# Attention tokens staged in natural order, one transfer per head, with the last 64 tokens of all heads in one transfer

## The chip, the core and the metric

The kernel runs on one core of a Trainium2 chip. The core has a matrix engine (PE, with its weight loads shown apart as PEld), a vector engine (DVE), a scalar engine for activations (ACT), a general engine (POOL), a sync engine that issues transfers (SP), and 16 DMA engines that every queue shares. Each engine works through its own instructions in the order in which they were written, and waits on semaphores of the others. The metric is the device time of one execution in microseconds.

## The reference

Two stages follow each other. Forgetting attention for 8 batches of 8 heads, 576 tokens and head size 64:

```
scores = (q @ k.T) / sqrt(64)
cum    = cumsum(log(clip(f, 1e-4, 1)))           # per head, over tokens
scores = where(causal, scores + cum[i] - cum[j], -1e9)
attn   = softmax(scores);  a = attn @ v
```

The heads are then put side by side (4608 tokens of 512), and go through a normalised gated feed-forward without biases:

```
xn  = x / sqrt(mean(x*x) + 1e-6) * rms_g
out = (silu(xn @ w_gate) * (xn @ w_val)) @ w_out       # 512 -> 1536 -> 512
```

All inputs and the output are float32.

## The kernel before

A batch is worked in four pairs of heads. Its 576 tokens are cut into five blocks, four of 128 and one of 64. For a pair, q and k of the first 512 tokens lie in `q32` and `k32` as [128, 2 heads, 4, 64], loaded so that partition p holds the four neighbouring tokens 4p to 4p+3, which is one run of 1 KB in memory for each head. The last 64 tokens of q and k lie in `r32` (q on partitions 0 to 63, k on 64 to 127), v in `v32` in natural order, partition p holding tokens p, 128+p and so on, in runs of 256 B. There are four sets of these tiles (NST = 4), so that a pair is loaded one batch ahead.

`cast` (L166) turns q, the rest and k into bfloat16 (`qkb`), on DVE in the first batch and on POOL in the others, and then issues the loads of the pair four further on. `scale_v` (L176) multiplies v with the decay factor of each key on POOL into `Vs`, and issues v's loads of the pair four further on. `transposes` (L187) turns the nine blocks of a pair with PE into one PSUM tile `tr`, in two parts, five blocks with the rest and then four of k; the tile exists once (`ps_tr` has one buffer), so the next transposes of any kind wait until DVE has copied it. That copy is L199: since block e holds every fourth token, it writes the 512 columns in the order (m e) while it reads them as (e m), with a stride of four in its destination. L202 copies the rest plainly, and two POOL copies (L204) build a block-diagonal matrix `QB` from it.

`scores` then multiplies q and k (L211), ACT exponentiates (L247), POOL masks (L215), and `values` multiplies with `Vs` (L273); DVE divides by the row sums (L276, L277) into `x`. The tile `po`, which holds these results and the scores of the last block (L225), also exists once. `squares` on ACT (L287), `root` on POOL (L293, L295), `normed` on DVE (L304) and `transpose_x` (L310 on PE, L317 on DVE, through the same `tr` tile) prepare the feed-forward. That is `gate` (L383, L386, L387), `value` (L393, L395) and `project` (L404, L410, store at L412), in groups of 512 tokens.

What sets the order is the function `order`: it issues the first batch alone, and after it a fixed list of the attention work of batch b+1 is dealt out among the feed-forward work of batch b, by counting. No engine reorders it. The decay factors come first: `decay_sums` (L144) clips f on DVE, takes the logarithm on ACT, scans on DVE and exponentiates on ACT; `decay_columns` (L153) transposes the result on PE, and DVE copies it to `decT`, which `scale_v` needs.

Transfers are issued on three queues. SP issues f, q and k, the later v and all stores of the output; ACT issues v of the first three pairs ahead of its first activation; POOL issues the weights, with a cast to bfloat16 on the way.

## Time and profile before

| | us |
|---|---|
| median of 2 runs | 504.88 |
| the runs | 502.15, 507.6 |
| the profiled execution | 507.5 |
| its span, from first to last instruction | 505.8 |

Its span by stage, from the busy time in windows:

| stage (us from the start) | PE busy | DVE busy | POOL busy | granted PE clock | DMA share |
|---|---|---|---|---|---|
| 0 to 12.6, first loads and decay | 0.00 | 4.09 | 0.73 | 1.00 | 0.83 |
| 12.6 to 57, batch 0 alone (two windows) | 23.98 | 26.27 | 25.07 | 1.00 | 0.79, 0.81 |
| 57 to 131, batch 0's feed-forward with batch 1 (two windows) | 59.78 | 47.01 | 36.19 | 1.00, 0.90 | 0.70, 0.57 |
| 185 to 239, a batch in mid-kernel | 46.54 | 34.92 | 21.84 | 0.94 | 0.31 |
| 294 to 346, another | 44.25 | 35.29 | 21.84 | 1.00 | 0.32 |
| 431 to 460, feed-forward alone | 28.95 | 17.54 | 0.00 | 1.00 | 0.10 |

Rows of the profile read thus. A group of instructions has its line, engine, operation, tiles (out<-in), shape and count, then busy time in all and the mean of one in ns, then the idle time of that engine just ahead of it and who ended it. In the chain of waits each line is a start, a duration and what ran; the chain is followed back from the last instruction to whatever released each step. A timeline row has start, duration, engine, line and operation, and in brackets the idle time before it with its releaser. Busy PE time is modelled, since matmuls are pipelined; a PE that idles is shown by its brackets.

### The profile page before, as it was taken

How to read it: one execution, taken by the hardware profiler on the slowest of the kernel's cores; microseconds unless marked ns; L12 is line 12 of the kernel's file. 1: busy time of each engine (PE TensorE's matmuls, PEld its weight loads, DVE VectorE, ACT ScalarE, POOL GpSimd, SP SyncE). 2: the span in 40 equal slices, each digit the busy share in tenths (PEclk: the TensorE clock that was granted, in tenths of full speed). 3: DMA queues.
4: the chain of work that ended last, by engine and by line, in shares of the span. 5: the costliest groups of instructions: out<-in, count | busy, mean ns of one | idle time of the engine just before them, and what ended most of it. 6: DMA issues, size and time to landing. Idle time of an engine off the chain costs nothing.

```text
span 505.8 us, 8861 instructions
## 1 busy us (share of the span) xinstructions
PE 414.6 (82%) x3317; PEld 205.5 (41%) x3317; DVE 312.7 (62%) x576; ACT 215.6 (43%) x354; POOL 175.7 (35%) x377
## 2 busy tenths in 40 slices
PE   0564677796989789879987898969897899999997
PEld 0343334343444344434443444434443444444443
DVE  3863487745686557773787368655866567374570
ACT  1443144562446235533546154634472454232331
POOL 0562636744344316351645034442544111000000
PEclk9999999997999799989999799999998999999999
DMA  8797839643052314331232305231000100201102
GB/s 214 197 204 125 163 91 189 164 116 113 25 138 72 92 62 128 86 93 56 80 112 60 103 25 139 71 113 43 2 0 23 64 1 0 85 0 38 46 2 83
DMA packets 75595, 43.20 MB, mean 85 GB/s; under 512 B 49888, under 2 KB 70880, under 8 KB 75552
## 3 DMA queue, kind: packets, MB, share of 16 engines
q1 hardware_dynamic: 67216, 37.03, 26.5%
q0 software_dynamic: 4736, 4.72, 6.0%
q10 hardware_dynamic: 3600, 0.89, 0.8%
q8 instruction: 26, 0.43, 0.3%
q14 instruction: 17, 0.14, 0.1%
HBM read 37.90 MB, written 9.44 MB: 94 GB/s over the span
## 4 chain that ended last, share of the span: by engine, by line
PE 56%; DVE 21%; ACT 10%; issue 6%; POOL 3%; DMA 2%; SPq 1%; POOLq 0%; ACTq 0%; DVEq 0%
PE bg L404 17%; PE bg L383 14%; PE bg L393 12%; DVE QK L199 5%; ACT junk L287 5%; PE po L273 5%; DVE th L387 4%; PE bg L211 4%; DVE xn L304 3%; ACT th L386 3%; DVE x L277 3%; DVE hT L395 3%; PE tr L310 3%; PE tr L194 1%; ACT PT L247 1%
## 5 line engine op out<-in xcount | busy, mean ns | idle before, releaser
L247 ACT ACTIVATE PT<-bg 128x1024 bf16<-128x1024 f32 x96 | 98.0, 1022 | 53.1 <-PE bg L211 52.9
L387 DVE SCALAR_TENSOR_TENSOR th<-th,bg 128x512 f32<-128x512 f32 x108 | 73.8, 683 | 63.9 <-ACT th L386 63.4
L393 PE MATMUL bg<-xT,wv 128*128 128x512 bf16 x432 | 113.0, 385 | 0.0
L404 PE MATMUL bg<-wo,hT 128*128 128x512 bf16 x432 | 111.6, 406 | 1.7 <-DVE hT L395 1.1
L383 PE MATMUL bg<-xT,wg 128*128 128x512 bf16 x432 | 112.8, 384 | 0.0
L386 ACT ACTIVATE th<-bg 128x512 f32<-128x512 f32 x108 | 64.4, 597 | 113.0 <-PE bg L383 113.0
L199 DVE COPY QK<-tr 128x512 bf16<-128x512 bf16 x64 | 83.0, 1297 | 11.3 <-PE tr L197 10.1
L395 DVE SCALAR_TENSOR_TENSOR hT<-th,bg 128x512 bf16<-128x512 f32 x108 | 74.4, 689 | 16.6 <-PE bg L393 9.0
L215 POOL TENSOR_SCALAR_AFFINE_SELECT PT<-PT 128x256 bf16<-128x256 bf16 (+1 forms) x96 | 46.6, 486 | 81.3 <-ACT PT L247 80.4
L404 PEld LDWEIGHTS <-hT 128*128 128x128 bf16 x432 | 41.7, 103 | 53.3 <-issue 11.8
L317 DVE TENSOR_SCALAR xT<-tr,rg 128x512 bf16<-128x512 bf16 (+7 forms) x64 | 20.6, 364 | 61.0 <-PE tr L310 61.0
L393 PEld LDWEIGHTS <-wv 128*128 128x128 bf16 x432 | 38.4, 99 | 43.7 <-issue 7.1
L194 PE MATMUL tr<-ident,qkb 128*128 128x128 bf16 x256 | 26.7, 231 | 35.7 <-DVE qkb L170 13.6
L383 PEld LDWEIGHTS <-wg 128*128 128x128 bf16 x432 | 37.9, 99 | 37.3 <-issue 1.7
L410 ACT COPY ores<-bg 128x512 f32<-128x512 f32 x36 | 21.1, 586 | 61.5 <-PE bg L404 61.5
L273 PEld LDWEIGHTS <-PT 128*128 128x128 bf16 x896 | 38.6, 104 | 19.3 <-POOL PT L215 5.2
L211 PE MATMUL bg<-QK 64*128 64x64 bf16 (+3 forms) x576 | 40.7, 251 | 0.0
L310 PE MATMUL tr<-ident,xn 128*128 128x128 bf16 x160 | 17.3, 243 | 28.0 <-DVE QK L199 19.5
L194 PEld LDWEIGHTS <-qkb 128*128 128x128 bf16 x256 | 18.7, 102 | 49.1 <-issue 21.8
L277 DVE TENSOR_TENSOR x<-po,rden 128x320 f32<-128x320 f32 x64 | 31.5, 492 | 2.2
L211 PEld LDWEIGHTS <-QK 64*128 64x128 bf16 x576 | 17.0, 98 | 28.6 <-issue 24.7
L310 PEld LDWEIGHTS <-xn 128*128 128x128 bf16 x160 | 12.8, 107 | 36.4 <-issue 21.7
(106 smaller groups left out, 323.4 us busy)
## 6 DMA issues: line engine op xcount, KB each, us to landing
out_dram<-ores SPq DMA_DIRECT2D x36, 256.0 KB, 2.0
q_0_103<-in_q_dram SPq DMA_DIRECT2D x8, 256.0 KB, 2.7
k_0_107<-in_k_dram SPq DMA_DIRECT2D x8, 256.0 KB, 3.2
q_1_104<-in_q_dram SPq DMA_DIRECT2D x8, 256.0 KB, 3.2
k_1_108<-in_k_dram SPq DMA_DIRECT2D x8, 256.0 KB, 3.3
q_2_105<-in_q_dram SPq DMA_DIRECT2D x8, 256.0 KB, 2.9
k_2_109<-in_k_dram SPq DMA_DIRECT2D x8, 256.0 KB, 3.4
q_3_106<-in_q_dram SPq DMA_DIRECT2D x8, 256.0 KB, 2.8
```

What stands on the lines that cost most here:

```text
L194: nc.tensor.transpose(tp[:, e * 128:(e + 1) * 128], src[:, 5 * part + e, :, :].rearrange("p h d -> p (h d)"), ident)
L199: nc.vector.tensor_copy(t[:, c:c + 512].rearrange("k (m e) -> k e m", e=4), tp[:, 0:512].rearrange("k (e m) -> k e m", e=4))
L211: nc.tensor.matmul(sc[:, par, c:c + n], lhsT=QK[b, p][rows, KEYS[kj]:KEYS[kj] + 128], rhs=QK[b, p][rows, q0:q0 + n], start=True, stop=True)
L247: nc.scalar.activation(t, sc, ACT.Exp, scale=scale)
L273: nc.tensor.matmul(po[:, qi, :], lhsT=weights_of(b, h, qi, kj), rhs=Vs[b % 2][:, kj, h, :], start=(kj == 0), stop=(kj == qi))
L277: nc.vector.tensor_tensor(xs[b][:, :, h * D:(h + 1) * D], po[:, :, 0:D], bcast(r[:, :], D), ALU.mult)
L383: nc.tensor.matmul(pg, lhsT=wg[:, dc, fc * 128:(fc + 1) * 128], rhs=xTs[g][:, dc, :], start=(dc == 0), stop=(dc == NDC - 1))
L386: readers[g, fc] = (nc.scalar.activation(t, pg, ACT.Tanh, scale=0.5), nc.vector.scalar_tensor_tensor(t, in0=t, scalar=1.0, in1=pg, op0=ALU ...
L387: nc.vector.scalar_tensor_tensor(t, in0=t, scalar=1.0, in1=pg, op0=ALU.add, op1=ALU.mult))
L393: beside(nc.tensor.matmul(pv, lhsT=wv[:, dc, fc * 128:(fc + 1) * 128], rhs=xTs[g][:, dc, :], start=(dc == 0), stop=(dc == NDC - 1)), reade ...
L395: nc.vector.scalar_tensor_tensor(hT, in0=ths.pop((g, fc)), scalar=0.5, in1=pv, op0=ALU.mult, op1=ALU.mult)
L404: beside(nc.tensor.matmul(po, lhsT=hTs[g, fc][:, j * 128:(j + 1) * 128], rhs=wo[:, fc, :], start=(fc == 0), stop=(fc == NFC - 1)), readers ...
```

## The change

Four things change together. q and k are loaded like v, in natural order: partition p holds tokens p, 128+p, 256+p and 384+p, in runs of 256 B, with one transfer for each head where there was one for a pair. The last 64 tokens of all eight heads come in one transfer for each of q, k and v (`load_last`), into `r32` and `s32`, of which there are two sets, one per batch in turn. v of the first batch is issued by POOL's queue and no longer by ACT and SP. And all loads of a pair are issued together behind its `scale_v`. With the tokens in natural order, a part's transposed blocks are copied out of PSUM by one plain copy of 640 or 512 columns. `scale_v` has one product per pair, and one more per batch for the last tokens of all heads. In `order`, the first pair's cast goes ahead of the decay sums and the second pair's behind the first V scaling.

```diff
--- before.py
+++ after.py
@@ -75,35 +75,38 @@
 
     q32 = [consts.tile([128, 2, 4, D], F32, name=f"q32_{i}") for i in range(NST)]
     k32 = [consts.tile([128, 2, 4, D], F32, name=f"k32_{i}") for i in range(NST)]
-    r32 = [consts.tile([128, 2, D], F32, name=f"r32_{i}") for i in range(NST)]
-    v32 = [consts.tile([128, NB, 2, D], F32, name=f"v32_{i}") for i in range(NST)]
+    v32 = [consts.tile([128, 2, 4, D], F32, name=f"v32_{i}") for i in range(NST)]
+    r32 = [consts.tile([128, H, D], F32, name=f"r32_{i}") for i in range(2)]
+    s32 = [consts.tile([64, H, D], F32, name=f"s32_{i}") for i in range(2)]
     Vs = [consts.tile([128, NB, H, D + 1], BF16, name=f"Vs{i}") for i in range(2)]
     PT4 = [consts.tile([128, 2, 128], BF16, name=f"PT4_{i}") for i in range(3)]
 
     QB = [consts.tile([128, 128], BF16, name=f"QB_{i}") for i in range(3)]
 
-    def load_qk(n):
+    def load_pair(n, what="qkv"):
 
         b, h0, i = n // NP, 2 * (n % NP), n % NST
-        for src, dst, r in ((q, q32[i], 0), (k, k32[i], 64)):
-            nc.sync.dma_start(out=dst.rearrange("p h e d -> p h (e d)"),
-                              in_=src[b, h0:h0 + 2, 0:512, :].rearrange("h (p e) d -> p h (e d)", e=4))
-            nc.sync.dma_start(out=r32[i][r:r + 64, :, :],
-                              in_=src[b, h0:h0 + 2, 512:S, :].rearrange("h p d -> p h d"))
-
-    def load_v(n, eng=nc.sync):
-        b, h0, i = n // NP, 2 * (n % NP), n % NST
-        for h in range(2):
-            eng.dma_start(out=v32[i][:, 0:4, h, :],
-                          in_=v[b, h0 + h, 0:512, :].rearrange("(j p) d -> p j d", p=128))
-        eng.dma_start(out=v32[i][0:64, 4, :, :],
-                      in_=v[b, h0:h0 + 2, 512:S, :].rearrange("h p d -> p h d"))
+        for name, src, dst in (("q", q, q32[i]), ("k", k, k32[i]), ("v", v, v32[i])):
+            for h in range(2 * (name in what)):
+                eng = nc.gpsimd if name == "v" and b == 0 else nc.sync
+                eng.dma_start(out=dst[:, h, :, :], in_=src[b, h0 + h, 0:512, :].rearrange("(j p) d -> p j d", p=128))
+
+    def load_last(b, what="qkv"):
+        for name, src, dst in (("q", q, r32[b % 2][0:64, :, :]), ("k", k, r32[b % 2][64:128, :, :]), ("v", v, s32[b % 2])):
+            if name in what:
+                eng = nc.gpsimd if name == "v" and b == 0 else nc.sync
+                eng.dma_start(out=dst, in_=src[b, :, 512:S, :].rearrange("h p d -> p h d"))
 
     fr = consts.tile([BH, NB * 128], F32)
     nc.sync.dma_start(out=fr[:, 0:S], in_=f.rearrange("b h s -> (b h) s"))
-    for n in range(NP):
-        load_qk(n)
-        load_v(n, nc.scalar if n < 3 else nc.sync)
+    load_pair(0, "qk")
+    load_last(0, "qk")
+    load_pair(0, "v")
+    load_pair(1, "qk")
+    load_last(0, "v")
+    load_pair(1, "v")
+    load_pair(2)
+    load_pair(3)
     rg = consts.tile([128, NDC], F32)
     with nc.allow_non_contiguous_dma(reason="512 gains, once"):
         nc.sync.dma_start(out=rg, in_=moe_rms_g.rearrange("(c p) -> p c", p=128))
@@ -167,22 +170,24 @@
         i = (b * NP + p) % NST
         t = qkb[b, p] = qbp.tile([128, 9, 2, D], BF16, name="qkb")
         eng = nc.vector if b == 0 else nc.gpsimd
-        eng.tensor_copy(t[:, 0:4, :, :].rearrange("p e h d -> p h e d"), q32[i])
-        eng.tensor_copy(t[:, 4, :, :], r32[i])
-        eng.tensor_copy(t[:, 5:9, :, :].rearrange("p e h d -> p h e d"), k32[i])
-        if b * NP + p + NST < B * NP:
-            load_qk(b * NP + p + NST)
+        eng.tensor_copy(t[:, 0:4, :, :].rearrange("p j h d -> p h j d"), q32[i])
+        eng.tensor_copy(t[:, 4, :, :], r32[b % 2][:, 2 * p:2 * p + 2, :])
+        eng.tensor_copy(t[:, 5:9, :, :].rearrange("p j h d -> p h j d"), k32[i])
 
     def scale_v(b, p):
-        i, h0 = (b * NP + p) % NST, 2 * p
+        n, h0 = b * NP + p, 2 * p
         if b > 1 and p == 0:
             nc.gpsimd.tensor_copy(Vs[b % 2][:, :, :, D], decT[:, :, b * H:(b + 1) * H])
-        for rows, j0, j1 in ((128, 0, 4), (64, 4, 5)):
-            dj = decT[0:rows, j0:j1, b * H + h0:b * H + h0 + 2]
-            nc.gpsimd.tensor_tensor(Vs[b % 2][0:rows, j0:j1, h0:h0 + 2, 0:D],
-                                    v32[i][0:rows, j0:j1, :, :], bcast(dj, D), ALU.mult)
-        if b * NP + p + NST < B * NP:
-            load_v(b * NP + p + NST)
+        dj = decT[:, 0:4, b * H + h0:b * H + h0 + 2].rearrange("p j h -> p h j")
+        nc.gpsimd.tensor_tensor(Vs[b % 2][:, 0:4, h0:h0 + 2, 0:D].rearrange("p j h d -> p h j d"),
+                                v32[n % NST], bcast(dj, D), ALU.mult)
+        if p == 0:
+            nc.gpsimd.tensor_tensor(Vs[b % 2][0:64, 4, :, 0:D], s32[b % 2],
+                                    bcast(decT[0:64, 4, b * H:(b + 1) * H], D), ALU.mult)
+        if n + NST < B * NP:
+            load_pair(n + NST)
+        if p == 0 and b > 0 and b + 1 < B:
+            load_last(b + 1)
 
     def transposes(b, p, part):
 
@@ -190,16 +195,12 @@
             QK[b, p] = qkt.tile([128, 9 * 128], BF16, name="QK")
         t, src = QK[b, p], qkb[b, p]
         tp = ps_tr.tile([128, NB * 128], BF16, name="tr")
-        for e in range(4):
-            nc.tensor.transpose(tp[:, e * 128:(e + 1) * 128],
-                                src[:, 5 * part + e, :, :].rearrange("p h d -> p (h d)"), ident)
+        c0, c1 = ((0, 5), (5, 9))[part]
+        for c in range(c0, c1):
+            nc.tensor.transpose(tp[:, (c - c0) * 128:(c - c0 + 1) * 128],
+                                src[:, c, :, :].rearrange("p h d -> p (h d)"), ident)
+        nc.vector.tensor_copy(t[:, c0 * 128:c1 * 128], tp[:, 0:(c1 - c0) * 128])
         if part == 0:
-            nc.tensor.transpose(tp[:, 512:640], src[:, 4, :, :].rearrange("p h d -> p (h d)"), ident)
-        c = 640 * part
-        nc.vector.tensor_copy(t[:, c:c + 512].rearrange("k (m e) -> k e m", e=4),
-                              tp[:, 0:512].rearrange("k (e m) -> k e m", e=4))
-        if part == 0:
-            nc.vector.tensor_copy(t[:, 512:640], tp[:, 512:640])
             for r in (0, 64):
                 nc.gpsimd.tensor_copy(QB[(b * NP + p) % 3][r:r + 64, r:r + 64], t[r:r + 64, 512:576])
 
@@ -434,14 +435,15 @@
 
     def order():
 
+        cast(0, 0)
         decay_sums()
-        cast(0, 0)
         transposes(0, 0, 0)
         transposes(0, 0, 1)
-        cast(0, 1)
         decay_columns()
         scale_v(0, 0)
+        cast(0, 1)
         scale_v(0, 1)
+        load_last(1)
         for i, works in enumerate(attention(0)):
             run(works)
             if i in (11, 20):
```

How the instructions stand is shown with the names of the tiles: `tr` is the PSUM tile of transposes, `QK` its copy, `th` and `hT` belong to the feed-forward, `decT` holds the decay columns, numbers are those of tiles, and line numbers after the change are those of the changed file (L202 is there the copy from `tr`, L388 and L396 what were L387 and L395).

On DVE in mid-kernel, between two pairs' scores, before:

```order
L199 COPY QK<-tr 128x4x128
L202 COPY QK<-tr 128x128
L395 SCALAR_TENSOR_TENSOR hT<-th,bg 128x512
L387 SCALAR_TENSOR_TENSOR th<-th,bg 128x512
L199 COPY QK<-tr 128x4x128 x2
L202 COPY QK<-tr 128x128
L395 SCALAR_TENSOR_TENSOR hT<-th,bg 128x512
```

and after:

```order
L202 COPY QK<-tr 128x640
L396 SCALAR_TENSOR_TENSOR hT<-th,bg 128x512
L388 SCALAR_TENSOR_TENSOR th<-th,bg 128x512
L202 COPY QK<-tr 128x512
L202 COPY QK<-tr 128x640
L396 SCALAR_TENSOR_TENSOR hT<-th,bg 128x512
```

The places stay; the first part of a pair has one copy where it had two, and no copy reorders.

On DVE at the start, from the end of the decay sums to the decay columns, before:

```order
L150 TENSOR_SCALAR mid<-mid 64x1
L170 CAST qkb<-q_0_103 128x2x4x64
L171 CAST qkb<-r_0_111 128x128
L172 CAST qkb<-k_0_107 128x2x4x64
L199 COPY QK<-tr 128x4x128
L202 COPY QK<-tr 128x128
L199 COPY QK<-tr 128x4x128
L170 CAST qkb<-q_1_104 128x2x4x64
L171 CAST qkb<-r_1_112 128x128
L172 CAST qkb<-k_1_108 128x2x4x64
L158 COPY decT<-po 128x320
```

and after, from the last cast of the first pair to the first of the second:

```order
L175 CAST qkb<-k_0_107 128x2x4x64
L148 MEMSET fr 64x64
L149 TENSOR_SCALAR fr<-fr 64x576
L151 SCALAR_TENSOR_TENSOR cum<-one,fr 64x576
L152 TENSOR_TENSOR mid<-cum 64x1
L153 TENSOR_SCALAR mid<-mid 64x1
L202 COPY QK<-tr 128x640
L202 COPY QK<-tr 128x512
L161 COPY decT<-po 128x320
L163 CAST Vs_119<-decT 128x40
L163 CAST Vs_120<-decT 128x40
L173 CAST qkb<-q_1_104 128x2x4x64
```

The decay sums moved behind the first pair's cast, which waits for loads, and the decay columns ahead of the second pair's cast.

On POOL at the start, before:

```order
masks.py:199 AFFINE_SELECT ident_f<-ident_f 128x128
L204 COPY QB_124<-QK 64x64 x2
L182 TENSOR_TENSOR Vs_119<-v_0_115,decT 128x4x2x64
L182 TENSOR_TENSOR Vs_119<-v_0_115,decT 64x2x64
L182 TENSOR_TENSOR Vs_119<-v_1_116,decT 128x4x2x64
L182 TENSOR_TENSOR Vs_119<-v_1_116,decT 64x2x64
```

and after:

```order
L92 DMA v_0_111<-in_v_dram 128x4x64
masks.py:199 ISA
masks.py:199 AFFINE_SELECT ident_f<-ident_f 128x128
L92 DMA v_0_111<-in_v_dram 128x4x64
L98 DMA s_0_117<-in_v_dram 64x8x64
L92 DMA v_1_112<-in_v_dram 128x4x64 x2
L92 DMA v_2_113<-in_v_dram 128x4x64 x2
L92 DMA v_3_114<-in_v_dram 128x4x64 x2
L205 COPY QB_124<-QK 64x64 x2
L182 TENSOR_TENSOR Vs_119<-v_0_111,decT 128x2x4x64
L185 TENSOR_TENSOR Vs_119<-s_0_117,decT 64x8x64
L182 TENSOR_TENSOR Vs_119<-v_1_112,decT 128x2x4x64
```

Nine issues of v stand ahead of POOL's first copy, the first of them ahead of the identity that the transposes use.

## The prediction

> **What bounds the kernel now.** I read the page first, then the groups by line and shape, the busy time by stage, the chain of waits, and last the timeline of single engines around the gaps that the chain showed.
>
> ```profile
> span 505.8 us, 8861 instructions
> PE 414.6 (82%) x3317; PEld 205.5 (41%) x3317; DVE 312.7 (62%) x576; ACT 215.6 (43%) x354; POOL 175.7 (35%) x377
> PE 56%; DVE 21%; ACT 10%; issue 6%; POOL 3%; DMA 2%; SPq 1%; POOLq 0%; ACTq 0%; DVEq 0%
> L199 DVE COPY QK<-tr 128x512 bf16<-128x512 bf16 x64 | 83.0, 1297 | 11.3 <-PE tr L197 10.1
> ...
> 239.00:294.00 55.00, 47.53 (x399) 23.53 (x398) 35.87 (x68) 25.10 (x42) 21.84 (x47) 0.94 0.30 85
> ```
>
> PE is busiest, but only 56% of the chain is PE; 21% is DVE, at 62% busy. DVE isn't full: PE waits because DVE works its queue in order and something slow stands ahead of what PE needs. The costliest thing there for its size is L199, the eviction of the transposes that also reorders columns: 1.297 us for 512 columns. In the row of a batch in mid-kernel (columns: PE, PEld, DVE, ACT, POOL busy, clock, DMA share, GB/s) DMA engines are 0.30 busy.
>
> The chain of one such batch, thinned to its L199 pieces and to one mark per batch (start, us, what), then the first and last L199 pieces of the whole chain:
>
> ```profile
> 240.50 0.69 DVE th L387
> ...
> 295.15 0.69 DVE th L387
> 295.83 0.06 DVE QK L199
> 295.89 0.97 issue
> ...
> 311.92 1.21 DVE QK L199
> ...
> 318.44 0.06 DVE QK L199
> ...
> 326.67 1.30 DVE QK L199
> ...
> 332.43 1.21 DVE QK L199
> ...
> 347.36 0.69 DVE th L387
> ...
> 27.86 1.20 DVE QK L199
> ...
> 401.58 0.06 DVE QK L199
> ```
>
> Five L199 lie on the path in each batch. The "issue" of 0.97 behind 0.06 is the same instruction: the next one on DVE begins only when L199 makes room. A batch takes 347.36 - 295.15 = 52.2 us, the one before it 295.15 - 240.50 = 54.65.
>
> **The change part by part.**
>
> *The copy from PSUM.* Natural token order needs no reordering, so a pair has one plain copy of 128x640 and one of 128x512 in place of two L199 and one L202. No row shows these shapes as a copy; the nearest are:
>
> ```profile
> L202 DVE COPY QK<-tr 128x128 bf16<-128x128 bf16 x32 | 7.9, 247 | 0.0
> ...
> L317 DVE TENSOR_SCALAR xT<-tr,rg 128x512 bf16<-128x512 bf16 x8 | 3.8, 480 | 2.8 <-PE tr L310 2.8
> ...
> L317 DVE TENSOR_SCALAR xT<-tr,rg 128x64 bf16<-128x64 bf16 x8 | 2.0, 247 | 7.0 <-PE tr L310 7.0
> ```
>
> L317 reads the same kind of tile plainly: (480 - 247)/448 = 0.52 ns a column. From L202, 512 columns cost 247 + 384 x 0.52 = 447 ns and 640 cost 513. A pair falls from 2 x 1297 + 247 = 2841 to 960 ns; 32 pairs free 60 us of DVE. Bounds of the copy: 447 ns, and 1297 if the order of columns is not what makes it slow. I take 447, nearest in tile, type and engine.
>
> Only what lies on the path counts. I count 35 places on the chain: 2 up to 57 us, 7 from 57 to 131, 25 in the five batches to 400, one at 401.58. Each gives 1297 - 447 = 0.85 us (at 326.67 the L202 goes too, which pays for its longer copy): 35 x 0.85 = 29.75 us. Does the wait there shrink by as much? Three of the places end in these rows:
>
> ```profile
> 298.26 0.23 PE L225 MATMUL po<-QB_125,QK 128*128 128x128 bf16 x1 [0.93 <-DVE x L277]
> ...
> 313.17 0.38 PE L194 MATMUL tr<-ident,qkb 128*128 128x128 bf16 x4 [1.52 <-DVE QK L199]
> ...
> 333.68 0.44 PE L310 MATMUL tr<-ident,xn 128*128 128x128 bf16 x5 [3.14 <-DVE QK L199]
> ```
>
> PE idles 0.93, 1.52 and 3.14 us, each over 0.85, so PE's own work doesn't catch the gain. What is late next: at 298.26 PE itself, 0.08 us on; at 333.68 still DVE. I take all of it; half is the lower bound (a rival).
>
> *The clock behind the long gap.* Half the clock is granted after some gaps:
>
> ```profile
> 100.58 0.58 PE L194 MATMUL tr<-ident,qkb 128*128 128x128 bf16 x4 [2.38 <-DVE QK L199]
> ...
> 118.92 0.69 PE L310 MATMUL tr<-ident,xn 128*128 128x128 bf16 x5 [3.81 <-DVE QK L199]
> ...
> 100.50:103.50 3.00, 2.92 (x13) 1.17 (x13) 1.38 (x3) 1.02 (x1) 0.51 (x3) 0.50 0.59 146
> 278.70:284.70 6.00, 6.00 (x33) 3.12 (x33) 1.33 (x4) 0.28 (x1) 0.29 (x1) 0.52 0.38 102
> 333.70:339.00 5.30, 5.30 (x54) 3.01 (x54) 1.88 (x6) 1.89 (x3) 0.32 (x2) 1.00 0.45 128
> ```
>
> The windows give PE, PEld, DVE, ACT, POOL, clock, DMA share and GB/s. The gap before L310 comes six times, at 118.92 with 3.81 us and then with 3.14; behind it the clock falls to 0.5 in five (row at 278.70), not in one (333.70). An episode costs 54.65 - 52.2 = 2.45 us. A 2.38 us gap at 100.58 was followed by 0.50 too; the 1.52 us gap at 313.17 by none. After the change the gap of 3.14 becomes 3.14 - 0.85 = 2.29 (the earlier L199 at 326.67 moves both its ends). That is nearest to the 2.38 that did fall, so most episodes stay: I let one of five go, 2.45 us. The gap of 2.38 becomes 1.53, like the harmless 1.52; half of the 2.9 us at half clock, 1.4, is saved. Bounds: all five go, 12.25; or a sixth comes, -2.45. I take 2.45 + 1.4 = 3.85.
>
> *Loads.* q and k come as 256 B reads instead of 1 KB, four times as many; per pair seven issues become six, and three per batch carry the last tokens.
>
> ```profile
> q1 hardware_dynamic: 67216, 37.03, 26.5%
> q0 software_dynamic: 4736, 4.72, 6.0%
> q10 hardware_dynamic: 3600, 0.89, 0.8%
> ...
> wg<-in_moe_w_gate_dram POOLq DMA_DIRECT2D x3, 512.0 KB, 7.1
> ...
> fr<-in_f_dram SPq DMA_DIRECT2D x1, 144.0 KB, 3.5
> ...
> 3.00:6.00 3.00, 0.00 (x0) 0.00 (x0) 0.58 (x2) 0.00 (x0) 0.00 (x0) 1.00 0.98 245
> L127 POOL DMA_DIRECT2D wg<-in_moe_w_gate_dram x3 | 2.6, 868 | 0.0
> ```
>
> q10 carries almost only 256 B reads of v: 0.008 x 16 x 505.8/3600 = 18 ns each. q1's mean is 31.9 ns, q0's (casting) 102. The profile thus prices a read of 256 B at 18 to 31.9 ns. A batch has 8192 reads of q and k and 5632 others: 13824 x 18/16 = 15.6 us of all engines, 27.6 by q1's mean, under a period of 52.2 - 5 x 0.85 = 48 us. Each load is issued a whole batch ahead of its use, so I cost them at nothing; that cover is gone only when loads of a batch take longer than the batch. Their issue now stands behind the V scaling on POOL rather than the casts, some 1 to 2 us later: hidden too. On SP they and the stores of the output still share one queue, and 6.75 issues per pair are no more than 7.
>
> *POOL.*
>
> ```profile
> L182 POOL TENSOR_TENSOR Vs_119<-v_0_115,decT 128x512 bf16<-128x512 f32 x4 | 4.2, 1054 | 2.7 <-issue 2.7
> ...
> L182 POOL TENSOR_TENSOR Vs_119<-v_0_115,decT 64x128 bf16<-64x128 f32 x4 | 1.6, 398 | 0.0
> ```
>
> Four times 1054 + 398 ns per batch become five of about 1054 (as an estimate, 64x512 at the price of 128x512): 5.8 to 5.3 us, 0.65 more at pair 0, 0.4 less at the others. POOL has 22 of 55 us to do: nothing.
>
> *Start-up.*
>
> ```profile
> 8.56 1.28 ACT L147 ACT_TABLE_LOAD   x1 [8.56 <-DMA v_1_116<-in_v_dram]
> 9.85 0.68 ACT L147 ACTIVATE fr<-fr 64x576 f32<-64x576 f32 x1
> ...
> 12.21 0.41 DVE L170 CAST qkb<-q_0_103 128x512 bf16<-128x512 f32 x1
> ...
> 18.01 1.40 POOL L182 TENSOR_TENSOR Vs_119<-v_0_115,decT 128x512 bf16<-128x512 f32 x2 [2.66 <-issue]
> ```
>
> Now ACT issues v until 8.56 and so begins the logarithm at 9.85; pair 0's cast waits on DVE behind the scan until 12.21. Afterwards ACT is free, the cast goes first, and the logarithm waits for it. Pair 0 needs fr and six transfers of 0.131 MB, 0.93 MB: with 0.8 us to the first issue, 2.9 of latency (fr's 3.5 less its 0.6 of transfer) and 245 GB/s, landing is at 7.5 if SP has the engines alone and 11.3 if POOL's v takes half. So the logarithm begins between 8.5 and 12.3. After it, the decay columns on DVE stand behind 0.96 us of copies where there were 2.84, and pair 1's three casts (0.41 for one) come behind them; but the first scores stand behind those casts on PE, so what V scaling gains the scores lose. Bounds -3 and +2.5 us; I take 0. POOL, with nothing else to do there, issues nine v transfers at about 0.87 us, 7.8 us; the last, out at 9, lands by 16 with wg's 7.1, before scaling begins at 18.01. The identity slips behind the first of them by 0.87 us; only the first transposes need it, and they wait for the loads.
>
> **The sum.** 29.75 + 3.85 = 33.6 us off. The profiled execution took 507.5 us, span 505.8: 472.2 and 473.9. The median of the runs is 2.6 lower, 504.88, which gives 471.3: I predict 471.5.
>
> **The rivals.**
>
> *All clock episodes vanish.* If a gap must be nearly as long as the six of 3.14 and more, 2.29 is too short. Then 4 x 2.45 = 9.8 more: 461.7. For it: only five of six fell even at 3.14; against it: 2.38 fell. The Trainium skill (TensorE: Matmul & The Clock Gate, the rules for kernel authors) asks only for no idle gap over about 3 us; the row at 100.58 disagrees.
>
> *The next wait takes half.* The mask on POOL, the squares on ACT or PE's own queue arrive just behind each L199. 35 x 0.425 less: 486.4. For it: at 298.26 only 0.08 us are to spare, and a batch has many such joints; against it: two of the three rows leave 0.67 and more.
>
> *The plain copy is no faster.* Should reading the PSUM tile set the 1297 ns, only the 1.4 us of the gap at 100.58 and less could be won: 503 to 505. Against it: L317.
>
> *256 B reads become the bound.* At x ns a read a batch's loads take 13824x/16. Six batches are loaded beside the work; to end over 515 each must grow from 48 to 55.3 us, so this decides from x = 64 ns, between q1's mean of 31.9 and q0's 102. At 75 ns a batch takes 64.8: 471.5 + 6 x 16.8 = 572. Against it: 18 ns on q10, measured while the engines were 0.98 busy. The Trainium skill (DMA: Bandwidth & Descriptors, Specifications) sets the smallest transfer at line rate at 512 B, which speaks against these reads; by its figure of about 27 GiB/s per engine the 18 ns would be half of line rate, so the trace agrees, and as an estimate from that page the sum would be the same.
>
> **How the numbers follow.** Forecast 0.50; no episodes 0.16; half caught 0.22; copy not faster 0.07; reads bind 0.05. Faster by over 2% (about what a measurement of this kernel can tell from no change) means under 494.8: 0.88; within 2% 0.07; slower 0.05. The range goes from 458 (no episodes and the good end of start-up) to 487 (half caught), leaving out the last two cases and the tails.
>
> **What would show it.** Right: copies of 0.45 and 0.51 us; DVE near 253 us busy; PE's wait before the L310 transposes near 2.3 us; batches of 48 us at full clock, 50 to 51 with an episode; batch 0's first scores within 2 us of now. Wrong: a DMA named as releaser of a cast in mid-kernel; POOL's masks releasing PE for over 0.5 us a batch; the first feed-forward matmul later than now. A copy over 0.6 us would break the largest term; a slow start only the smallest.

## The result, and the profile after

The changed kernel takes 470.79 us (median of two runs, both 470.79) where the kernel before takes 504.88: a ratio of 0.9325, with a 95% interval from 0.9108 to 0.9542. The forecast was 471.5 within 458 to 487, and faster. The profiled execution took 470.79 too, with a span of 468.8 us where 505.8 stood: 37.0 us less.

The page of the changed kernel, with the lines that answer to those of before (the last gives the granted clock in tenths, slice by slice):

```profile
span 468.8 us, 8739 instructions
PE 400.8 (85%) x3317; PEld 201.1 (43%) x3317; DVE 262.3 (56%) x544; ACT 214.1 (46%) x354; POOL 179.1 (38%) x362
...
PEclk9996589998999999999999999999999999999999
```

The groups by line and shape for the new copies (count, busy us and mean ns, idle before):

```profile
L202 DVE COPY QK<-tr 128x640 bf16<-128x640 bf16 x32 | 15.6, 486 | 10.2 <-PE tr L200 10.2
L202 DVE COPY QK<-tr 128x512 bf16<-128x512 bf16 x32 | 13.3, 416 | 0.7 <-PE tr L200 0.7
```

The copies take 486 and 416 ns where 513 and 447 were forecast, and DVE is busy for 262.3 us where it was 312.7. The copies' own sum fell further, from 90.9 to 28.9 us. A long copy's last 0.2 us lies beside the next instruction (before, the copy at 326.67 takes 1.30 and the next begins at 327.76), and of that hidden part there is now less: hence 262 and not the 253 that was forecast (15.9 us of the 90.9 were hidden so, 6.3 of the 28.9 are). PE is busy 85% of the span, and from 120 us on every slice has full clock.

The slices of half clock from 35 to 70 us are no loss against before, although the page of before shows full clock there. PE's timeline of the kernel before has the same slow matmuls at the start of its feed-forward:

```profile
57.60 1.91 PE L383 MATMUL bg<-xT,wg 128*128 128x512 bf16 x4
...
62.67 1.03 PE L393 MATMUL bg<-xT,wv 128*128 128x512 bf16 x4
```

After, four of these matmuls take 1.91 us at 58.19 and 1.03 at 62.74. The trace of before holds no clock record ahead of 62.60 us, so the 1.00 in its table for the stretches up to there was not measured.

The chain of waits of the changed kernel, thinned (start, us, what): one wait in the first batch, then one batch in mid-kernel with its two marks and the longer of its copies:

```profile
83.29 5.74 DMA v_3_114<-in_v_dram
...
220.25 0.69 DVE th L388
...
235.87 0.34 DVE QK L202
...
249.35 0.48 DVE QK L202
...
254.32 0.34 DVE QK L202
...
254.70 0.44 PE tr L311 x5
...
268.38 0.69 DVE th L388
```

From mark to mark the batch takes 48.13 us, against 54.65 and 52.2 before; 48 was forecast. The copies stand at the same five places of the chain as before, each shorter.

Where the span went is read from the ACT copies of output rows (L411, `ores`): the fourth of each batch is a mark, seen in both traces. Of the 37.05 us by these marks (36.95 of the whole span), 7.13 lie in the stretch to the first (128.46 before, 121.33 after), 29.12 in the five batches that follow, and 0.80 in what is behind them. The five batches gave 6.59, 6.54, 6.51, 4.07 and 5.41. The fourth is the clean price of the copies, since it had full clock before and after: 52.21 to 48.14. What the other four gave above 4.07, together 8.77 us, came from half clock that is gone.

### The profile page after: what moved, and what is told of

It reads as the page before. It is cut to its first block, busy times and chain, and to the rows that moved or that the text cites. A ratio compares the mean times of both kernels' runs of the same rounds, so it can differ in the third digit from the quotient of the medians.

```text
span 468.8 us, 8739 instructions
## 1 busy us (share of the span) xinstructions
PE 400.8 (85%) x3317; PEld 201.1 (43%) x3317; DVE 262.3 (56%) x544; ACT 214.1 (46%) x354; POOL 179.1 (38%) x362
## 4 chain that ended last, share of the span: by engine, by line
PE 63%; DVE 17%; ACT 6%; POOL 4%; issue 4%; SPq 3%; DMA 2%; POOLq 0%; DVEq 0%; ACTq 0%
PE bg L384 16%; PE bg L405 16%; PE bg L394 15%; PE po L274 5%; PE bg L212 4%; DVE xn L305 4%; DVE th L388 3%; DVE x L278 3%; SPq L92 3%; ACT th L387 3%; DVE hT L396 2%; PE tr L311 2%; PE tr L200 2%; ACT junk L288 2%; DVE QK L202 2%
## 5 line engine op out<-in xcount | busy, mean ns | idle before, releaser
L388 DVE SCALAR_TENSOR_TENSOR th<-th,bg 128x512 f32<-128x512 f32 x108 | 74.2, 687 | 81.6 <-ACT th L387 81.4
L387 ACT ACTIVATE th<-bg 128x512 f32<-128x512 f32 x108 | 64.4, 596 | 106.1 <-PE bg L384 103.7
L384 PE MATMUL bg<-xT,wg 128*128 128x512 bf16 x432 | 112.2, 383 | 0.0
L405 PE MATMUL bg<-wo,hT 128*128 128x512 bf16 x432 | 102.3, 383 | 2.0 <-DVE hT L396 2.0
L216 POOL TENSOR_SCALAR_AFFINE_SELECT PT<-PT 128x256 bf16<-128x256 bf16 (+1 forms) x96 | 47.6, 495 | 92.3 <-ACT PT L248 91.2
L396 DVE SCALAR_TENSOR_TENSOR hT<-th,bg 128x512 bf16<-128x512 f32 x108 | 74.0, 685 | 10.3 <-PE bg L394 2.3
L405 PEld LDWEIGHTS <-hT 128*128 128x128 bf16 x432 | 39.9, 98 | 46.8 <-issue 3.6
L384 PEld LDWEIGHTS <-wg 128*128 128x128 bf16 x432 | 37.8, 99 | 37.2 <-issue 1.4
L200 PE MATMUL tr<-ident,qkb 128*128 128x128 bf16 x288 | 28.8, 229 | 28.7 <-DVE QK L202 8.2
L411 ACT COPY ores<-bg 128x512 f32<-128x512 f32 x36 | 21.1, 585 | 55.0 <-PE bg L405 55.0
L274 PEld LDWEIGHTS <-PT 128*128 128x128 bf16 x896 | 36.6, 101 | 18.9 <-POOL PT L216 6.0
L200 PEld LDWEIGHTS <-qkb 128*128 128x128 bf16 x288 | 21.1, 102 | 41.6 <-issue 16.6
L202 DVE COPY QK<-tr 128x640 bf16<-128x640 bf16 x64 | 28.9, 451 | 10.9 <-PE tr L200 10.9
L311 PE MATMUL tr<-ident,xn 128*128 128x128 bf16 x160 | 16.3, 233 | 20.4 <-DVE QK L202 12.0
L274 PE MATMUL po<-Vs_119,PT 128*128 128x65 bf16 x448 | 22.2, 204 | 5.1 <-POOL PT L216 3.7
```

The costliest lines, as they stand in the source:

```text
L200: nc.tensor.transpose(tp[:, (c - c0) * 128:(c - c0 + 1) * 128], src[:, c, :, :].rearrange("p h d -> p (h d)"), ident)
L216: nc.gpsimd.affine_select(out=d, in_=d, pattern=pattern, compare_op=ALU.is_ge, fill=0.0, base=0, channel_multiplier=-1)
L274: nc.tensor.matmul(po[:, qi, :], lhsT=weights_of(b, h, qi, kj), rhs=Vs[b % 2][:, kj, h, :], start=(kj == 0), stop=(kj == qi))
L384: nc.tensor.matmul(pg, lhsT=wg[:, dc, fc * 128:(fc + 1) * 128], rhs=xTs[g][:, dc, :], start=(dc == 0), stop=(dc == NDC - 1))
L387: readers[g, fc] = (nc.scalar.activation(t, pg, ACT.Tanh, scale=0.5), nc.vector.scalar_tensor_tensor(t, in0=t, scalar=1.0, in1=pg, op0=ALU ...
L388: nc.vector.scalar_tensor_tensor(t, in0=t, scalar=1.0, in1=pg, op0=ALU.add, op1=ALU.mult))
```

## Experiments

Times are compared with runs of the kernel before on the same chip, whose medians were 500.68, 502.35, 500.83 and 503.94 us in the four sets. "Feed-forward start" is the first matmul of L384; where its row counts three of the four matmuls, the record of the first is missing and I take the start 0.43 us earlier, which is the distance of these matmuls. The first matmul of the value product then follows 1.71 us behind, as it does in the kernel before (57.60 and 59.31).

### The copies alone, and the rest alone

The first run puts the reordering copies of before back into the changed kernel; the output's tokens are then out of place, while the work stays the same.

```diff
-        nc.vector.tensor_copy(t[:, c0 * 128:c1 * 128], tp[:, 0:(c1 - c0) * 128])
+        c = c0 * 128
+        nc.vector.tensor_copy(t[:, c:c + 512].rearrange("k (m e) -> k e m", e=4),
+                              tp[:, 0:512].rearrange("k (e m) -> k e m", e=4))
         if part == 0:
+            nc.vector.tensor_copy(t[:, 512:640], tp[:, 512:640])
```

> The changed kernel with the old copies put back: 512 columns reordered, the rest copied apart, so q and k of this run are scrambled over tokens; all loads, casts and orders stay as changed. Theory 1 (the plain copy carries nearly all of the gain, the clock episodes follow from the gap that it shortens): L199-like copies of 1.30 us, batches of 52 to 55 us, the gap before the transposes of x back at about 3.1 us with half clock behind most of them, 500 to 508 us in all. Rival (merged transfers and the order of issue carry a part of the 34 us): under 495 us.

The second puts the plain copies into the kernel before, loads and order as they were.

```diff
-        nc.vector.tensor_copy(t[:, c:c + 512].rearrange("k (m e) -> k e m", e=4),
-                              tp[:, 0:512].rearrange("k (e m) -> k e m", e=4))
+        w = 640 if part == 0 else 512
+        nc.vector.tensor_copy(t[:, c:c + w], tp[:, 0:w])
         if part == 0:
-            nc.vector.tensor_copy(t[:, 512:640], tp[:, 512:640])
```

> The kernel before with only the copies made plain (640 and 512 columns); loads, casts, scaling and order stay as before, and the tokens of q and k stay interleaved, so that masks fall on other tokens. Theory 1: batches of 48.1 us as in the changed kernel, and the feed-forward begins 2 to 3 us earlier than there (its start-up lost to the loads): 466 to 469 us. Rival (the new loads gain something themselves): 474 us or more. Second rival (start-up is bound by something else than the loads): 470 to 472.

Measured: 506.23 us for the first (ratio 1.0099, 1.0066 to 1.0131), with copies of 1294 ns, gaps of 3.15 us ahead of the next batch's transposes and half clock behind four of the five. 467.14 us for the second (0.9306, 0.925 to 0.9363), with batches of 48.1 us. So the plain copy carries the whole gain, and everything else in the change together costs about 1%, less than the 2% that the prediction took for what a measurement of this kernel can tell from no change. The batches of 48.1 us are the same with the old loads and the new ones; what the rest costs must lie in the first part, where the feed-forward starts at 59.48, 1.88 us later than before, with the old copies in both. The second run and the changed kernel are the cleaner pair, since both have full clock in all five batches: the feed-forward starts at 54.80 and 58.19, the first mark stands at 118.59 and 121.33, and behind it no stretch differs by more than 0.1 us. So the rest of the change costs 2.74 us up to the first mark and nothing behind it.

### The gap and the clock

Before, a gap of 3.14 us at the turn of a batch was followed by half clock in four of five batches. The forecast gap was 2.29 us. These rows are PE's timeline of the changed kernel; the bracket is the idle time ahead and what ended it:

```profile
112.56 0.44 PE L311 MATMUL tr<-ident,xn 128*128 128x128 bf16 x5 [2.94 <-DVE QK L202]
...
249.49 1.46 PE L405 MATMUL bg<-wo,hT 128*128 128x512 bf16 x6 [0.18 <-DVE hT L396]
...
251.43 1.47 PE L405 MATMUL bg<-wo,hT 128*128 128x512 bf16 x6
254.70 0.44 PE L311 MATMUL tr<-ident,xn 128*128 128x128 bf16 x5 [1.81 <-DVE QK L202]
```

The gap is 1.80 or 1.81 us, not 2.29, and no half clock follows. Was the reason right and only the length wrong? To tell, spare DVE work was put at the place where it lengthens only this gap, in four sizes. In each, the edit is this one with another number of columns or products:

```diff
+    spare = consts.tile([128, DM], BF16, name="spare")
...
+            if b > 0 and j == NB - 1:
+                for i in range(1):
+                    nc.vector.tensor_scalar_mul(spare[:, 0:400], x[:, 0:400], r)
```

400 columns, once:

> The changed kernel with one spare product of 400 columns on DVE behind the last normed row of batches 1 to 7, about 0.45 us, just ahead of the copy that releases the transposes of x. The gap of 1.8 us becomes about 2.27, the length that the prediction gave it. If such a gap trips the clock in most cases, as the prediction took it: 7 x 0.45 and four more episodes of 2.45, about 483 us. If the gap must be near 3 us: 473 to 475 us, granted clock 1.0 in mid-kernel.

512 columns, twice:

> The same with two spare products of 512 columns, about 1.13 us in all: a gap of about 2.9 us. Theory (the length of the gap decides): five or so episodes of 2.45 us and 7 x 1.13: 486 to 493 us, clock 0.5 behind the gaps. Rival (the phase of the batch period against the clock's window decides, not the gap): no episodes in mid-kernel, 478 to 480 us.

264 columns, once:

> The changed kernel with one spare DVE product of 264 columns behind the last normed row of batches 1 to 7, so that the gap ahead of the next batch's first transposes comes out near the 2.29 us that the prediction forecast (2.52 us with 400 columns, 1.80 with none). If such a gap trips the clock as the longer ones do, some of the five batches are followed by matmuls at half clock, a batch with one lasts about 50.2 us, and the time is 475 to 480. If 2.29 us is still under the limit, all five periods are 48.13 us plus the added 0.4 to 0.5, and the time is 473.5 to 475.

48 columns, once:

> As the run with a spare product of 264 columns, with 48 in its place. That one lengthened the gap to 2.45 us and not to 2.29: 264 columns added 0.65 us, 400 added 0.72, so that most of a product's price is fixed, and 48 should add about 0.55 and give 2.35 us, or as little as 0.15 if the short product finds a free moment. If the limit lies between 1.80 and 2.35 us, one or two of the five batches are again followed by half clock, with periods near 50.3 us, and the time is 475 to 480. If it lies between 2.35 and 2.45, all five periods are 48.2 to 48.7 and the time is 471.5 to 475.

PE's timeline of the run with 48 columns, two batches that follow each other:

```profile
260.26 0.44 PE L316 MATMUL tr<-ident,xn 128*128 128x128 bf16 x5 [2.33 <-DVE QK L202]
...
261.00 1.46 PE L410 MATMUL bg<-wo,hT 128*128 128x512 bf16 x6
...
308.91 0.44 PE L316 MATMUL tr<-ident,xn 128*128 128x128 bf16 x5 [2.33 <-DVE QK L202]
...
309.64 2.35 PE L410 MATMUL bg<-wo,hT 128*128 128x512 bf16 x6
```

The same gap, 2.33 us, and the same six matmuls behind it: 1.46 us the first time, 2.35 the second. From turn to turn a batch takes 48.65 us without half clock and 50.33 with it. All the runs together:

| gap | batches followed by half clock | time, us |
|---|---|---|
| 1.80 (the changed kernel) | 0 of 5 | 470.79 |
| 2.33 (48 columns) | 2 of 5 | 478.61 |
| 2.45 (264 columns) | 2 of 5 | 480.29 |
| 2.52 (400 columns) | 3 of 5 | 480.71 |
| 3.10 (512 columns twice) | 4 of 5 | 486.26 |
| 3.14 (the kernel before) | 4 of 5 | 504.88 |
| 3.15 (the old copies put back, above) | 4 of 5 | 506.23 |

Only the middle four differ from the changed kernel by spare work alone; the last two times have the old copies in them. The run with 400 columns was meant for 2.27 us and came to 2.52; its 480.71 us lie between its two expectations, 473 to 475 and about 483. The run with twice 512 came out as the first of its theories expected. The run with 264 columns missed the 2.29 us that it was meant for, and its time is 0.3 us over the expected 475 to 480; the run with 48 came to 2.33 and 478.61, as expected if the limit lies below 2.35. With 400 columns a batch takes 50.5 us with half clock and 48.85 without, with twice 512 some 51.07 and 49.4. A longer gap trips the clock more often, but none of these lengths is a sharp limit. The one gap of 2.94 us in the first batch shows it best: it is followed by half clock in the changed kernel and not in a faster variant below, at the same length. So length alone does not decide, as the rival of the run with twice 512 columns had it in part.

The traces show what does. Within each of them, every change of the granted clock falls on a raster of 3.41 us. In the run with 48 columns half clock lasts from 211.07 to 214.49 and from 310.06 to 313.47, and the two starts lie 29 steps apart. These are four windows of that raster (stretch, length, then busy time of PE, PEld, DVE, ACT and POOL, granted clock, DMA share, GB/s):

```profile
207.66:211.07 3.41, 1.14 (x22) 0.93 (x22) 2.85 (x9) 0.56 (x1) 1.85 (x2) 1.00 0.94 215
211.07:214.49 3.42, 3.42 (x10) 1.31 (x9) 0.57 (x2) 0.28 (x1) 0.29 (x1) 0.50 0.29 96
255.44:258.85 3.41, 2.33 (x18) 1.17 (x18) 3.38 (x9) 1.61 (x2) 3.33 (x6) 1.00 0.20 45
258.85:262.27 3.42, 2.01 (x26) 1.33 (x26) 2.59 (x7) 0.00 (x0) 0.99 (x2) 1.00 1.03 254
```

The gap that ends at 209.93 lies in one window, which leaves PE idle for 2.27 us of it, and the next window has half clock. The equal gap that ends at 260.26 is split between two windows, idle for 1.08 and 1.41 us, and the clock stays. The same count over all thirteen traces from 63 us on, by PE's modelled busy time: 30 windows at full clock had over 2.05 us of idle PE, and half clock followed each of them; of the more than 1400 with under 1.95 us none was followed by it; of five in between, two were. So what looks like chance is the place of the gap in the raster. A gap of 1.80 us cannot fill a window far enough wherever it falls, and none of the 35 such gaps in seven kernels was followed by half clock. One of 2.33 us can. As an estimate from 3.41 us and a limit of 2.0, (3.41 + gap - 4.0)/3.41 of all places trip the clock: 0.51 at 2.33 us, 0.74 at 3.10.

The Trainium skill (TensorE: Matmul & The Clock Gate, Part 1) calls its activity window free-running; the raster, which starts elsewhere in each trace, agrees. The Trainium skill's rule for kernel authors (the same title, "Why this matters for your kernels") of no idle gap over about 3 us is too lax here: 2.33 us cost a batch 1.68 us in two of five cases.

Why was the gap 1.80? PE's timeline of the kernel before, around the same turn:

```profile
326.85 1.46 PE L404 MATMUL bg<-wo,hT 128*128 128x512 bf16 x6
...
328.79 1.75 PE L404 MATMUL bg<-wo,hT 128*128 128x512 bf16 x6
```

and DVE's there, the instruction for which the last of these matmuls waited:

```profile
329.42 0.67 DVE L395 SCALAR_TENSOR_TENSOR hT<-th,bg 128x512 bf16<-128x512 f32 x1
```

and DVE's after:

```profile
251.30 0.67 DVE L396 SCALAR_TENSOR_TENSOR hT<-th,bg 128x512 bf16<-128x512 f32 x1
```

Before, hT was done at 330.09 and PE's last six matmuls at 330.54, 0.45 behind it: PE waited for DVE. After, hT is done at 251.97 and the matmuls at 252.90, 0.93 behind: PE works through without a wait, 1.47 us for six. Measured from the first block of six, hT comes 3.24 us behind its start before (326.85 to 330.09) and 2.48 after (249.49 to 251.97), but PE's end moved only from 3.69 to 3.41. The shorter copy brings DVE 0.76 us forward there and PE 0.28, and the gap loses that difference, 0.48, besides the 0.86 of its own copy: 3.14 - 1.34 = 1.80.

### The opening

Four runs separate what the change does before the first feed-forward. The first restores the opening order of before:

```diff
-        cast(0, 0)
         decay_sums()
+        cast(0, 0)
         transposes(0, 0, 0)
         transposes(0, 0, 1)
+        cast(0, 1)
         decay_columns()
         scale_v(0, 0)
-        cast(0, 1)
```

> The changed kernel with the opening's order of before: the decay sums first, and both casts of the first heads ahead of the decay columns; loads and copies stay those of the changed kernel. If the order is what makes the opening late (the decay sums, and with them the logarithm, stand behind a cast that waits 4.99 us for r's transfer), the logarithm goes back from 12.78 to about 10, the first feed-forward matmul from 58.19 to 56 or less, and the time to 467.5 to 469. If the reads of 256 bytes or the Pool queue's v hold the data back, the first scores wait for the same transfers as now: the first feed-forward matmul at 57.5 to 58.5, the time 470 to 471.

The second takes v of the first batch off POOL's queue (the same line in `load_pair` and `load_last`):

```diff
-                eng = nc.gpsimd if name == "v" and b == 0 else nc.sync
+                eng = nc.sync
```

> The changed kernel with v of the first batch issued by SyncE, at the same place in the order of issue, so that one queue carries everything. If the Pool queue's v takes DMA engines from q, k and r in the first 20 us, r lands earlier, the first feed-forward matmul is at 55 to 56.5, and the time is 467 to 469. If the reads of 256 bytes are the cause, nothing is gained, since the same bytes are read in the same packets: 57.5 to 59 and 470 to 472. A loss is possible too: SyncE has then more transfers to issue ahead of the second heads' q and k, and at 0.7 us for each of them the first feed-forward matmul would be at 59 to 60, the time 471.5 to 473.

The third has both edits:

> Both edits of the two runs above in one kernel. If order and Pool queue are the whole of the opening's loss, the first feed-forward matmul is at 55 or earlier and the time at 466 to 467.5, as in the kernel before with the plain copies alone (467.14). If the reads of 256 bytes are most of it, 469 to 471.

The fourth reads q and k in runs of 1 KB, in the changed kernel:

```diff
-                eng.dma_start(out=dst[:, h, :, :], in_=src[b, h0 + h, 0:512, :].rearrange("(j p) d -> p j d", p=128))
+                if name == "v":
+                    eng.dma_start(out=dst[:, h, :, :], in_=src[b, h0 + h, 0:512, :].rearrange("(j p) d -> p j d", p=128))
+                else:
+                    eng.dma_start(out=dst[:, h, :, :].rearrange("p e d -> p (e d)"),
+                                  in_=src[b, h0 + h, 0:512, :].rearrange("(p e) d -> p (e d)", e=4))
```

> The changed kernel with q and k read in runs of 1 KB (four tokens in a row to a partition) and the plain copies kept, so that the masks and the columns of the sequence stand in another order of tokens: the output is not the reference's. Opening order and Pool queue stay as in the changed kernel. If the 256-byte reads hold the opening back, the first feed-forward matmul is at 55 to 56 and the time at 467 to 468.5; if the order or the Pool queue does, 57.5 to 58.5 and 470 to 471. In the middle of the kernel both theories expect the same batches of 48.1 us, since the loads lie a batch ahead.

A fifth, later, joins the last two:

> Order and Pool queue undone together, as in the kernel that took 464.0 us, and q and k read in runs of 1 KB besides; the masks and the sequence's columns stand in another order of tokens, so that the output is not the reference's. If the 256-byte reads cost the opening something that the two other causes covered, the first feed-forward matmul comes ahead of 52.45 us by 1 us or more and the time is 462 to 463. If they cost nothing, 52 to 53 us and 463.5 to 465.

DVE's timeline of the changed kernel shows the wait that starts it:

```profile
11.81 0.23 DVE L174 CAST qkb<-r_0_115 128x128 bf16<-128x128 f32 x1 [4.99 <-DMA r_0_115<-in_k_dram]
```

and ACT's what stands behind it, the logarithm and the first exponential of scores:

```profile
12.78 0.68 ACT L150 ACTIVATE fr<-fr 64x576 f32<-64x576 f32 x1 [10.70 <-DVE fr L149]
...
22.21 1.02 ACT L248 ACTIVATE PT<-bg 128x1024 bf16<-128x1024 f32 x1 [4.84 <-PE bg L212]
```

The same places in the run with both edits, DVE:

```profile
8.08 0.23 DVE L174 CAST qkb<-r 128x128 bf16<-128x128 f32 x1 [0.99 <-DMA r<-in_k_dram]
```

and ACT:

```profile
4.16 0.68 ACT L150 ACTIVATE fr<-fr 64x576 f32<-64x576 f32 x1 [2.08 <-DVE fr L149]
...
12.14 1.02 ACT L248 ACTIVATE PT<-bg 128x1024 bf16<-128x1024 f32 x1 [3.40 <-PE bg L212]
```

With the changed order the first cast stands ahead of the decay sums on DVE, and it waits for r; ACT, idle since its table load at 0.8 us, waits 10.70 us with it. With v on POOL's queue r comes at 11.81 us; without it, at 8.1 to 8.4. SP issues r at the same time in both. This is the second of r's two issues in SP's timeline, first of the changed kernel, then of the run with both edits:

```profile
4.40 0.67 SPq L98 DMA_DIRECT2D r_0_115<-in_k_dram  x1
...
4.37 0.64 SPq L98 DMA_DIRECT2D r<-in_k_dram  x1
```

and this its row in the lists of the transfers of the first 20 us, in the same order (number, size, us from issue to landing):

```profile
r_0_115<-in_k_dram SPq DMA_DIRECT2D x1, 128.0 KB, 7.3
...
r<-in_k_dram SPq DMA_DIRECT2D x1, 128.0 KB, 3.6
```

So r isn't issued late; beside POOL's v its transfer takes 3.7 us longer. The columns are the starts of the rows named, in us:

| kernel | cast of r | logarithm | first exponential | feed-forward start | time (ratio, interval) |
|---|---|---|---|---|---|
| before | 12.54 | 9.85 | 18.36 | 57.60 | 504.88 |
| changed | 11.81 | 12.78 | 22.21 | 58.19 | 470.79 (0.9325, 0.9108 to 0.9542) |
| old order | 11.56 | 4.52 | 16.02 | 55.85 | 468.93 (0.9341, 0.9308 to 0.9375) |
| v by SyncE | 8.37 | 9.34 | 18.77 | 54.63 | 467.57 (0.9317, 0.9287 to 0.9347) |
| both | 8.08 | 4.16 | 12.14 | 52.02 | 464.0 (0.925, 0.922 to 0.928) |
| 1 KB reads | 10.66 | 11.77 | 21.19 | 57.77 | 470.52 (0.9374, 0.9335 to 0.9414) |
| both, 1 KB reads | 7.86 | 4.17 | 11.74 | 50.83 | 462.15 (0.9233, 0.9216 to 0.9249) |

The order costs 2.34 us of feed-forward start, POOL's v 3.56, both 6.17, a little more than their sum. Both single runs came out in time as their theories expected, at 468.93 and 467.57; but the logarithm came earlier, at 4.52 and not near 10, since ACT has no v to issue any more, and without POOL's v the feed-forward starts at 54.63, a little ahead of the 55 to 56.5 that was expected. So the opening is held by the order and by v on POOL's queue, each for its part. "Both" beats the kernel before and the changed one; it beats its two halves on the same chip beyond their intervals, and was faster than expected (464.0 against 466 to 467.5), because it doesn't restore the opening of before but combines ACT's freedom from issuing with the early logarithm.

Read size: here the theory of 256-byte reads fell. With 1 KB reads in the changed kernel the first exponential comes 1.0 us earlier, and the feed-forward only 0.4; where the rest goes was not followed, and the time is the same. With the other two causes gone, 1.2 us of feed-forward start are seen, and 462.15 us against 464.0, though these two were timed on different chips and their intervals overlap. These 1.2 us, all in the opening, are what shorter reads cost here, and nothing in batches loaded ahead (48.1 us with both). The Trainium skill (DMA: Bandwidth & Descriptors, Specifications) wants 512 B for line rate.

## Why the prediction was right, and where errors cancelled

**The copy: right.** The price was forecast within 31 ns, and on the chain 4.07 us a batch came where five places of 0.85 make 4.25. At 4.07/5 the 35 places are worth 28.5 us, 29.75 forecast. Order of columns, not the PSUM tile, made the old copy slow, as the second run shows. The rivals "plain copy no faster" and "next wait takes half" fall with it: POOL's masks are nowhere in the chain of the batch from 220.25 to 268.38.

**The clock: the step that failed.** "The gap of 3.14 becomes 3.14 - 0.85 = 2.29 (the earlier L199 at 326.67 moves both its ends)". It moved DVE's end by 0.76 us and PE's by 0.28, since PE stopped waiting for hT and was held by its own matmuls. The reading of the threshold, "most episodes stay" at 2.29, held in part: at 2.33 us the clock still falls, but in two of five batches and not in most, since length alone is no limit and the place in the 3.41 us raster decides with it. At 1.80 it never falls, so the term was 8.77 us in the five batches where 2.45 was forecast. The rival "all episodes vanish" came true for the four in these batches, though for another reason than the one given for it; behind the first batch's gap, 3.81 us before and 2.94 after, half clock stays. Its 461.7 us were not reached, because the episodes were worth 8.77 us and not 12.25, and the copies and the stretch to the first mark gave less than their terms. The other gap, 2.38 forecast to become 1.53, became 1.52, with no half clock behind it.

**The opening: the term mis-sized.** Taken as 0 between -3 and +2.5; the feed-forward starts 1.88 us later with the old copies in both kernels and 3.39 later with the plain ones in both, of which 2.74 are left at the first mark, a little over the upper bound. The step "what V scaling gains the scores lose" failed in its first half. V scaling gained nothing: it begins at 18.95 where it began at 18.01, because the logarithm came at 12.78, past the 8.5 to 12.3 that was forecast. Landing was forecast at 7.5 or, "if POOL's v takes half", 11.3; r came at 8.1 without POOL's v and at 11.8 with it, so both ends were well sized and the second was the true one. The first scores were to come within 2 us of before, and came 3.85 later; the first feed-forward matmul came 0.6 later, one of the signs named against the forecast.

**Loads and POOL in mid-kernel: right,** at nothing: 48.1 us a batch with old and new loads. A DMA does stand in the chain once, for 5.74 us at 83.29, where the chain names v_3 as what a cast on POOL waited for, during batch 0's feed-forward. It wasn't there before; the variant with both edits has it too (5.75 us). The trace shows no cost: POOL's mask ahead of that cast waits for ACT, starts at 88.68 and takes 0.41, and the cast starts at 89.03 without idle time. The rival of reads that bind is refuted by DMA engines 0.40 busy from 220 to 268 us.

**The sum.** To the first mark 9.05 forecast (nine places at 0.85 and 1.4 of clock), 7.13 measured; the five batches 23.70 (21.25 and 2.45) and 29.12; the end 0.85 and 0.80. So the 33.6 became 37.05: the clock gave 6.3 more than its term in the batches, the copies 0.9 less there and the stretch to the first mark 1.9 less. These errors leave the sum 3.45 us short. That the time was still met within 1 us has one more cause: the forecast was taken from the median before, 504.88, which lies 2.6 us under the profiled execution against which the 37.05 are counted. Such a near hit is luck; the range, and not the last digit, is what the working could carry.

What stays open: the first run is 5.5 us slower than the kernel before, and its later feed-forward explains 1.88; the rest wasn't followed through the half-clock batches, which differ from run to run in both kernels. How v on POOL's queue slows r, in the engines or behind them, was not told apart either.

## What to carry to other kernels

When a delay on one engine is shortened, ask for both ends of each idle gap behind it what holds them now: one end may be held by the other engine's own work already, and then the gap shrinks by more, or less, than the edit. Before an instruction that waits for a transfer is moved ahead in a queue, list what stands behind it on that engine and which other engines those feed; here one early cast held ACT for 10.70 us. And a queue that was idle isn't free in an opening: v on POOL's queue made r land 7.3 us after its issue and not 3.6, so the data that is needed last should not be issued beside the data that is needed first.

## What the runs showed of the hardware

The granted clock changes on a raster of 3.41 us, and half clock follows a window of it in which PE idled for over about 2 us (30 of 30 over 2.05, none under 1.95). So a gap trips it by its length and its place: in none of five at 1.80 us, two at 2.33 and 2.45, three at 2.52, four at 3.10. An episode of one window cost 1.62 to 1.68 us in the runs with spare work. In the kernel before, three of the five batches had episodes of two windows, 6.83 us, and these cost 2.44 to 2.52; six matmuls took 2.75 and 2.36 us there, against 1.46.

A copy out of PSUM with its columns strided by four at the destination cost 1297 ns for 512 columns of bf16, the plain one 416.

SP's issues grew while POOL's queue held v. In SP's timeline of the changed kernel (two issues to a row):

```profile
10.21 2.63 SPq L92 DMA_DIRECT2D q_2_105<-in_q_dram  x2
12.88 3.10 SPq L92 DMA_DIRECT2D k_2_109<-in_k_dram  x2
```

and of the run with both edits:

```profile
10.33 1.05 SPq L92 DMA_DIRECT2D q<-in_q_dram  x2
```

With 1 KB reads and v still on POOL's queue, the same two took 1.56 and 1.42 us, and the feed-forward came only 0.4 us earlier. r, which holds up the opening, is issued ahead of these and at the same time with and without POOL's v, so the longer issues are not what makes it late.
